# Softmax sums and running maxima on VectorE, taken over two columns of one operand in place of two operands

## The chip, the cores and the metric

The kernel runs on one core of a Trainium2 chip. A core has a matrix engine (TensorE, PE in the profile, with its weight loads as PEld), VectorE (DVE), ScalarE (ACT), GpSimd (POOL) and a queue that issues DMAs (SP). All work on SBUF, the core's memory of 128 partitions; TensorE writes to PSUM, which VectorE and ScalarE read. The metric is the device time of one execution in microseconds (us).

## The reference

Sliding-window attention with four sink tokens, over 4 batches, 8 heads, 768 positions and head size 64, followed by a soft mixture of experts over the 3072 tokens: 8 experts with 4 slots each.

```
scores = scale * q @ k^T
keep   = (key is one of the first 4) or (0 <= query - key < 128)
scores = where(keep, scores, -1e9)
a = exp(scores - max(scores))
a = a / (sum(a) + 1e-9)
x = a @ v                                   # 3072 tokens of 512

logits = x @ phi                            # 3072 x 32
d = exp(logits - logits.max(0));  d /= d.sum(0) + 1e-9
slot_out = relu(d^T @ x, per expert, @ w1) @ w2
c = exp(logits - logits.max(1));  c /= c.sum(1) + 1e-9
out = c @ slot_out
```

Two softmaxes matter here: that of the attention, one sum per query and head, and that over the tokens (`d`), whose maximum and sum run along as the tokens are made.

## The kernel before

The attention is cut into 12 jobs of 256 queries (4 batches times 3). Each job loads its keys, queries and values, transposes keys and queries on TensorE, and then works on four tiles; a tile covers 128 rows of queries (half of each 128) and four heads. For each tile, in `softmax`: TensorE makes the scores `s` in PSUM, VectorE masks them and takes the negated maxima `nm`, ScalarE takes the exponentials of the four heads in four instructions, each of which also reads out its sum, and VectorE makes the reciprocals: it adds the constant 1e-9 to the four sums (`inverse`, a `tensor_tensor` with the four-column tile `eps`) and inverts. GpSimd then multiplies the weights `pt` by them. TensorE transposes `pt`, ScalarE or VectorE copies the result out (`xw`), GpSimd's `affine_select` cuts it to the window, and TensorE multiplies by the values.

Each job then passes its 256 tokens on to `Moe.tokens`, the softmax over tokens with a running maximum: `logits` on TensorE, their maximum on VectorE (`new`, one column of the pair `m`, which alternates between jobs), the smaller of the new and the old negated maximum, exponentials on ScalarE, and then the running sum `z`, which VectorE multiplies by the factor `al` and to which it adds the job's own sum `zb` (`totals`). `slot_softmax` runs once a batch over `call`, the logits of that batch's tokens; its maxima are `rm` and its sums `rs`. After the last job come the two expert layers, whose weights are loaded from early on, and the output.

The order on each engine is fixed when the program is built. Each step is given to a list scheduler (`Plan.add`) with a key, an engine and an estimated time; the scheduler's order is the order in which each engine runs its instructions, and an engine waits at each instruction for what that instruction needs. Nearly every recorded instruction has line 127, the helper that records it, so the names of its tiles tell instructions apart: `wt<-wt 128x4` on VectorE are the attention's sums and reciprocals, since `wt` is the name of the shared slots in which `pt`, `small` and `eps` lie; `sums` is the tile that holds `m`, `z`, `zb` and `al`; `first` holds keys and queries, and the tokens `x` with their transposes.

Of the kernel before, what the change touches and what calls it, by code (L numbers as in the profile page):

```python
# [14 lines left out]
ALU = mybir.AluOpType  # L15
AX = mybir.AxisListType
# [6 lines left out]
EPS = 1e-9  # L23
# [254 lines left out]
class Moe:  # L278
# [27 lines left out]
    def tokens(self, plan, keys, b, j, x, xn, blocks):  # L306

        nc, c = self.nc, self.c
        n, self.n = self.n, self.n + 1
        old, new = self.m[:, (n + 1) % 2:(n + 1) % 2 + 1], self.m[:, n % 2:n % 2 + 1]
        lt, z, acc, xt = self.lt, self.z, self.acc, self.xt
        al, zb = (x[:, n % 2:n % 2 + 1] for x in (self.al, self.zb))
        aln, zbn = ("al", n % 2), ("zb", n % 2)
        lb, lg = self.lb[:, n % 2], self.call[:, b, 2 * j:2 * j + 2]
        both = len(blocks) == 2
        k = iter(keys)  # L320
        L, T, S = plan.psum(), plan.psum(), plan.psum()

        xs = [("xt", b, u) for b in blocks for u in range(2)]

        def logits(e):
            for a in range(4):
                for g in range(4):
                    nc.tensor.matmul(L["tile"][32 * g:32 * g + 32, 0:P], lhsT=c.phi[:, a, :],
                                     rhs=xt[:, a, x[g % 2 if both else blocks[0]]], start=(a == 0), stop=(a == 3),
                                     skip_group_check=True)  # L330

        plan.add(next(k), "P", 0.87, logits, r=xs + ["phi"], w=[L["name"]], new=L, mode=(128, 32))

        key = next(k)
        plan.add(key, "V", 0.2, lambda e: nc.vector.tensor_reduce(
            new, L["tile"][:, 0:P], op=ALU.max, axis=AX.X, negate=True), r=[L["name"]], w=[("m", n % 2)])
        if n:
            plan.add(key, "V", 0.07, lambda e: nc.vector.tensor_tensor(new, new, old, op=ALU.min),
                     r=[("m", (n + 1) % 2)], w=[("m", n % 2)])
        plan.add(next(k), "A", 0.16, lambda e: nc.scalar.copy(lt[0:64], L["tile"][0:64, 0:P]), r=[L["name"]], w=["lt0"])  # L340
        plan.add(next(k), "A", 0.34,
                 lambda e: nc.scalar.activation(lt[64:128], L["tile"][64:128, 0:P], AF.Exp, bias=new[64:128],
                                                accum_out=zb[64:128]),
                 r=[L["name"], ("m", n % 2)], w=["lt1", zbn], last=L)
        if n:

            plan.add(next(k), "A", 0.19,
                     lambda e: nc.scalar.activation(al, old, AF.Exp, bias=new, scale=-1.0),
                     r=[("m", 0), ("m", 1)], w=[aln])
        else:  # L350
            next(k)
        plan.add(next(k), "P", 0.11, lambda e: nc.tensor.transpose(T["tile"][:, 0:P], lt, c.ident),
                 r=["lt0", "lt1"], w=[T["name"]], new=T)
        i = slice(0, 2) if both else slice(blocks[0], blocks[0] + 1)

        def natural(e, w):
            t = T["tile"][:, 0:P].rearrange("p (w i s) -> p w i s", w=2, i=2)
            o, t = (lb, t[:, 1]) if w else (lg[:, i], t[:, 0, i])
            (nc.scalar.copy if e == "A" else nc.vector.tensor_copy)(o, t)

        plan.add(next(k), "AV", (0.1, 0.13), lambda e: natural(e, 1), r=[T["name"]], w=[("lb", n % 2)])
        logit = lambda e: natural(e, 0)

        def products(e):
            for g in range(4):
                i, o = g % 2, slice(256 * (g // 2), 256 * (g // 2) + 256)
                if both:
                    lhs, rhs = lb[:, i, :], xn[i][:, o]
                else:
                    rows = slice(64 * i, 64 * i + 64)  # L370
                    lhs, rhs = lb[rows, i, :], xn[blocks[0]][rows, o]
                nc.tensor.matmul(S["tile"][32 * g:32 * g + 32, 0:256], lhsT=lhs, rhs=rhs, start=True, stop=True)

        plan.add(next(k), "P", 0.45, products, r=[("lb", n % 2)] + [("xn", b) for b in blocks], w=[S["name"]], new=S,
                 mode=(128, 32))

        def sums(e):
            if n:
                nc.vector.scalar_tensor_tensor(acc, acc, al, S["tile"][:, 0:256], op0=ALU.mult, op1=ALU.add)
            else:  # L380
                nc.vector.tensor_copy(acc, S["tile"][:, 0:256])

        def totals(e):
            if not n:
                nc.vector.tensor_copy(z[64:128], zb[64:128])
            elif both:
                nc.vector.scalar_tensor_tensor(z[64:128], z[64:128], al[64:128], zb[64:128],
                                               op0=ALU.mult, op1=ALU.add)
            else:
                nc.vector.tensor_tensor(z[64:128], z[64:128], al[64:128], op=ALU.mult)  # L390
                nc.vector.tensor_tensor(z[64:96], z[64:96], zb[64:96], op=ALU.add)

        plan.add(next(k), "V", 0.14, totals, r=[zbn, aln], w=["z"])
        key = next(k)
        plan.add(next(k), "AV", (0.1, 0.13), logit, r=[T["name"]], w=[("lg", b, j, x) for x in blocks], last=T)
        plan.add(key, "V", 0.4, sums, r=[S["name"], aln], w=["acc"], last=S)
# [259 lines left out]
def window_path(ctx, tc, c, moe, q, k, v, phi, w1, w2, out):  # L656
# [6 lines left out]
    nc = moe.nc = Core(tc)  # L663
    B, H, S, D = q.shape
    NJ = S // 256
    plan = Plan(moe.pools)
# [5 lines left out]
    def slot():  # L672
        return slots.tile([P, 2048], F32, name="wt")

    t, u = moe.first
# [7 lines left out]
    t = slot()  # L683
# [3 lines left out]
    t = slot()  # L687
    pts = [t[:, 528 * i:528 * i + 528].rearrange("p (a y) -> p a y", a=4) for i in range(PT)]
    skb = t[:, 1584:1840].rearrange("p (i r h s) -> p i r h s", i=2, r=4, h=H)
    small = t[:, 1840:1864].rearrange("p (g x y) -> p g x y", g=3, x=2)  # L690
    eps = t[:, 1864:1868]
    v4s.append(t[:, 1868:1932])
    qt = fr.tile([P, 4, 256], F32, name="qt")
    vsink = fr.tile([P, 4, P], F32R, name="vsink")
    pst = fr.tile([P, 256], F32R, name="pst")
    nc.vector.memset(eps, EPS)

    jobs = [(b, j) for b in range(B) for j in range(NJ)]
    N = len(jobs)
# [75 lines left out]
    def softmax(keys, n, tl):  # L775

        b, j = jobs[n]
        g = 4 * n + tl
# [3 lines left out]
        nm, z = small[:, g % 3, 0], small[:, g % 3, 1]  # L782
# [43 lines left out]
        def exps(e):  # L826
            for a in range(4):
                nc.scalar.activation(pt[:, a, :], used[0][:, a % 2, a // 2, :], AF.Exp, bias=nm[:, a:a + 1],
                                     accum_out=z[:, a:a + 1])

        add(keys["E"], "A", 1.42, exps, r=[sn, nn], w=[pn, zn], last=s)

        def inverse(e):
            nc.vector.tensor_tensor(z, z, eps, op=ALU.add)
            nc.vector.reciprocal(z, z)

        add(keys["N"], "V", 0.33, inverse, r=[zn], w=[zn])
        add(keys["N"], "G", 1.08, lambda e: nc.gpsimd.tensor_tensor(
            pt, pt, z.unsqueeze(2).to_broadcast([P, 4, 132]), op=ALU.mult), r=[zn, pn], w=[pn])
# [297 lines left out]
def fused(ctx, tc, q, k, v, n_sink, window, phi, w1, w2, out):  # L1137
# [42 lines left out]
    with tc.If(flag == 1) as cmp:  # L1180
        with ExitStack() as c2:
            window_rest(tc, moe, *window_path(c2, tc, c, moe, q, k, v, phi, w1, w2, out), out)
# [33 lines left out]
```

## Time and profile before

| | |
|---|---|
| time, median of 3 runs | 254.32 us (253.89 to 254.34) |
| profiled execution, span | 252.0 us |
| mean granted clock of TensorE in it | 0.966 |
| instructions on VectorE, busy | 445, 171.3 us |
| instructions on GpSimd, busy | 281, 143.2 us |
| loaded and stored | 59.38 MB |

The page gives the profiled execution by its span, from the first to the last instruction; the runs' times are taken of the whole execution, and are 2.3 us above it in the median. The twelve jobs run from about 9 us to 196 us; every third job begins a batch, and one batch takes about 44 us. The expert layers and the output take the rest.

The costliest groups of GpSimd, and the two groups of VectorE that are largest (columns: line, engine, operation, written and read tiles, shapes, count; busy us and mean ns of one; idle time of the engine before them and what ended it):

```profile
L127 POOL TENSOR_TENSOR wt<-wt 128x528 f32<-128x528 f32 (+1 forms) x96 | 64.4, 677 | 14.4 <-DVE wt L127 8.4
L127 POOL TENSOR_SCALAR_AFFINE_SELECT wt<-wt 128x512 f32<-128x512 f32 x88 | 53.6, 638 | 20.8 <-DVE wt L127 12.0
L127 DVE TENSOR_REDUCE wt<-s 128x4 f32<-128x528 f32 x48 | 34.0, 707 | 1.7
L127 DVE COPY_PREDICATED s<-later,s 128x256 f32<-128x256 uint8 x48 | 20.3, 423 | 2.7 <-PE s L127 2.0
```

Busy time of an engine counts from an instruction's start to its end, and so also what it stands still in between; idle time is what lies between instructions.

### The profile page before, as it was taken

To read this page: it belongs to the slowest core of one execution; us is meant where nothing else is said; L and a number is where in the kernel's file an instruction comes from. 1 tells how busy PE (TensorE), PEld (TensorE's weight loads), DVE (VectorE), ACT (ScalarE), POOL (GpSimd) and SP (SyncE) were. 2 spreads that over 40 slices of the span, in tenths; PEclk is the share of its full clock that TensorE was granted. 3 is DMA by queue.
4 is the path that set the end of the run, shared out by engine and by line. 5 is a ranking of instruction groups with operands and counts; after the bars stand their busy time and mean duration, and the time that the engine had idled before them with its cause. 6 is when DMAs were issued, how large, how long until landed. Compare 5 with 4: busy or idle time off the path is not lost.

```text
span 252.0 us, 7482 instructions
## 1 busy us (share of the span) xinstructions
PE 225.1 (89%) x2754; PEld 162.0 (64%) x2754; DVE 171.3 (68%) x445; ACT 143.7 (57%) x568; POOL 143.2 (57%) x281
## 2 busy tenths in 40 slices
PE   7969899989998999999899899998999999997900
PEld 7746677857786786778678677876677434335800
DVE  3297879788889978888997888898554413104810
ACT  2368887558786665879666587975545112103700
POOL 2038897955958596595859659596884060000000
PEclk9979999999999999999999999999999999998865
DMA  5597899799799799969988982640159999950995
GB/s 117 111 205 171 172 290 275 239 275 283 232 217 257 229 300 272 279 218 208 271 314 217 279 252 50 137 151 5 37 193 347 349 414 423 410 213 23 388 395 207
DMA packets 84495, 59.38 MB, mean 236 GB/s; under 512 B 76260, under 2 KB 76260, under 8 KB 82916
## 3 DMA queue, kind: packets, MB, share of 16 engines
q1 hardware_dynamic: 84452, 58.83, 78.1%
q8 instruction: 24, 0.39, 0.6%
q14 instruction: 19, 0.16, 0.2%
HBM read 52.53 MB, written 6.29 MB: 233 GB/s over the span
## 4 chain that ended last, share of the span: by engine, by line
PE 56%; DVE 22%; ACT 9%; issue 5%; POOL 2%; DVEq 0%; ACTq 0%; POOLq 0%
PE w L127 42%; PE s L127 13%; DVE wt L127 10%; ACT wt L127 7%; DVE s L127 7%; POOL wt L127 2%; PE w L1168 2%; DVE sums L127 1%; DVE rs L127 1%; DVE call L127 1%; ACT lt L127 1%; DVE acc L127 1%; DVE wt L579 0%; ACT qt L127 0%; ACT wt L578 0%
## 5 line engine op out<-in xcount | busy, mean ns | idle before, releaser
L127 POOL TENSOR_TENSOR wt<-wt 128x528 f32<-128x528 f32 (+1 forms) x96 | 64.4, 677 | 14.4 <-DVE wt L127 8.4
L127 ACT ACTIVATE wt<-s,wt 128x132 f32<-128x132 f32 x192 | 68.4, 386 | 6.9 <-DVE wt L127 6.1
L127 POOL TENSOR_SCALAR_AFFINE_SELECT wt<-wt 128x512 f32<-128x512 f32 x88 | 53.6, 638 | 20.8 <-DVE wt L127 12.0
L127 PE MATMUL w<-wt 128*64 128x128 f32 (+3 forms) x550 | 51.9, 320 | 1.6 <-DVE wt L579 1.5
L127 PEld LDWEIGHTS w<-wt 128*64 128x64 f32 (+2 forms) x550 | 37.3, 144 | 13.5 <-DVE wt L579 2.2
L127 PE MATMUL s<-wt,qt 64*64 64x196 f32 (+2 forms) x768 | 41.4, 327 | 4.2 <-ACT wt L127 3.2
L127 PE MATMUL w<-ident,first 128*128 128x128 f32 x288 | 41.6, 281 | 2.4 <-DVE acc L127 1.3
L127 ACT ACTIVATION_READ_ACCUMULATOR wt<-s,wt 128x1 f32 x192 | 42.6, 222 | 0.0
L127 ACT COPY wt<-w 128x512 f32<-128x512 f32 x45 | 26.6, 595 | 25.5 <-PE w L127 22.1
L127 PE MATMUL w<-ident,wt 128*128 128x128 f32 x250 | 39.0, 283 | 1.6 <-ACT lt L127 0.8
L127 PEld LDWEIGHTS w<-ident,first 128*128 128x128 f32 x288 | 31.8, 142 | 9.7 <-issue 3.9
L127 PEld LDWEIGHTS s<-wt,qt 64*64 64x64 f32 x768 | 26.6, 134 | 14.7 <-issue 7.4
L127 DVE TENSOR_REDUCE wt<-s 128x4 f32<-128x528 f32 x48 | 34.0, 707 | 1.7
L127 PEld LDWEIGHTS w<-ident,wt 128*128 128x128 f32 x250 | 27.9, 146 | 9.9 <-POOL wt L127 2.9
L127 DVE TENSOR_TENSOR wt<-wt 128x4 f32<-128x4 f32 x48 | 16.4, 342 | 12.0 <-ACT wt L127 11.1
L127 ACT COPY first<-w 128x512 f32<-128x512 f32 x31 | 17.9, 596 | 8.4 <-PE w L127 8.2
L127 DVE COPY_PREDICATED s<-later,s 128x256 f32<-128x256 uint8 x48 | 20.3, 423 | 2.7 <-PE s L127 2.0
L127 DVE COPY wt<-w 128x512 f32<-128x512 f32 x27 | 18.3, 679 | 2.1 <-PE w L127 1.7
L127 PE MATMUL w<-first,phi 128*32 128x128 f32 x384 | 13.1, 276 | 2.0 <-DVE first L127 1.9
L127 POOL COPY wt<-wt 128x512 f32<-128x512 f32 (+2 forms) x13 | 5.8, 455 | 15.0 <-ACT wt L127 14.9
L127 PE MATMUL w<-wt,si 128*32 128x512 f32 x128 | 13.9, 593 | 0.2 <-DVE si L127 0.2
L127 PE MATMUL s<-wt 128*32 128x512 f32 (+1 forms) x144 | 14.0, 498 | 0.0
(116 smaller groups left out, 240.8 us busy)
## 6 DMA issues: line engine op xcount, KB each, us to landing
wt<-in_moe_w_dram SPq DMA_DIRECT2D x30, 1024.0 KB, 7.4
wt<-in_v_dram SPq DMA_DIRECT2D x24, 256.0 KB, 4.9
first<-in_k_dram SPq DMA_DIRECT2D x22, 256.0 KB, 3.7
first<-in_q_dram SPq DMA_DIRECT2D x22, 256.0 KB, 4.4
out_dram<-wt SPq DMA_DIRECT2D x5, 1024.0 KB, 8.3
first<-in_moe_w_dram SPq DMA_DIRECT2D x2, 1024.0 KB, 5.0
out_dram<-wt SPq DMA_DIRECT2D x2, 512.0 KB
first<-in_k_dram SPq DMA_DIRECT2D x4, 128.0 KB, 2.3
```

The lines of the kernel that those rows point to most:

```text
L127: return self.tc.keep_in_program_order(f(*args, **kw))
L1168: nc.tensor.matmul(t[:, 0:P], lhsT=c.ident, rhs=c.ident, start=True, stop=True)
```

## The change

Three operations of VectorE are written in another form; what is computed stays the same.

1. The attention's sums. ScalarE writes its sums into a new tile `ze`, which has two columns for each sum: the sum itself and, set once, the constant 1e-9. VectorE sums both columns of each pair with one `reduce_sum` (8 values in, 4 out), in place of adding the tile `eps` to the tile of sums. This occurs 48 times, once a tile.
2. The running maximum. The smaller of the two negated maxima is taken by one `tensor_reduce` over both columns of `m`, in place of a `tensor_tensor` of the two columns. This occurs 11 times.
3. The running sum. `z * al + zb` is one `tensor_scalar` with two scalars per partition, in place of a `scalar_tensor_tensor` whose addend is a tensor. This occurs 11 times.

```diff
-            plan.add(key, "V", 0.07, lambda e: nc.vector.tensor_tensor(new, new, old, op=ALU.min),
+            plan.add(key, "V", 0.07, lambda e: nc.vector.tensor_reduce(new, self.m, op=ALU.min, axis=AX.X),
                      r=[("m", (n + 1) % 2)], w=[("m", n % 2)])
...
-                nc.vector.scalar_tensor_tensor(z[64:128], z[64:128], al[64:128], zb[64:128],
-                                               op0=ALU.mult, op1=ALU.add)
+                nc.vector.tensor_scalar(z[64:128], z[64:128], al[64:128], zb[64:128], op0=ALU.mult, op1=ALU.add)
...
     small = t[:, 1840:1864].rearrange("p (g x y) -> p g x y", g=3, x=2)
-    eps = t[:, 1864:1868]
+    ze = t[:, 1932:1956].rearrange("p (g y e) -> p g y e", g=3, e=2)
...
-    nc.vector.memset(eps, EPS)
+    nc.vector.memset(ze[:, :, :, 1], EPS)
...
                 nc.scalar.activation(pt[:, a, :], used[0][:, a % 2, a // 2, :], AF.Exp, bias=nm[:, a:a + 1],
-                                     accum_out=z[:, a:a + 1])
+                                     accum_out=ze[:, g % 3, a, 0:1])
...
         def inverse(e):
-            nc.vector.tensor_tensor(z, z, eps, op=ALU.add)
+            nc.vector.reduce_sum(z, ze[:, g % 3], axis=AX.X)
             nc.vector.reciprocal(z, z)
```

The keys and the estimated times of the steps are as before, and with them the order on all engines. As an example, VectorE's instructions around a slot softmax, first before the change (`rm`, `call` and `rs` are of the slot softmax, the rows `wt<-wt 128x4` of the attention's sums):

```order
L127 TENSOR_REDUCE rm<-call 128x6
L127 TENSOR_TENSOR call<-call,rm 128x192
L127 TENSOR_TENSOR wt<-wt 128x4
L127 RECIPROCAL wt<-wt 128x4
L127 COPY first_77<-w 128x512
L127 COPY wt<-w 128x2x4x64
```

At the same place with the change, on VectorE too:

```order
L127 TENSOR_REDUCE rm<-call 128x6
L127 TENSOR_TENSOR call<-call,rm 128x192
L127 TENSOR_REDUCE wt<-wt 128x4
L127 RECIPROCAL wt<-wt 128x4
L127 COPY first_77<-w 128x512
L127 COPY wt<-w 128x2x4x64
```

Nothing has moved; one row has another operation.

## Prediction

> **What bounds the kernel now.** I read the page first, then the windows, then the instructions in order of time.
>
> ```profile
> span 252.0 us, 7482 instructions
> PE 225.1 (89%) x2754; PEld 162.0 (64%) x2754; DVE 171.3 (68%) x445; ACT 143.7 (57%) x568; POOL 143.2 (57%) x281
> PE 56%; DVE 22%; ACT 9%; issue 5%; POOL 2%; DVEq 0%; ACTq 0%; POOLq 0%
> ```
>
> TensorE holds 56% of the chain that ended last, VectorE 22%. Where VectorE's part lies is told by the windows (busy us of each engine in a stretch).
>
> ```profile
> core 0: us, PE busy (x) PEld busy (x) DVE busy (x) ACT busy (x) POOL busy (x), PEclk, DMA share, GB/s
> 58.50:73.90 15.40, 15.40 (x211) 12.51 (x213) 13.39 (x32) 11.97 (x52) 11.64 (x21) 1.00 0.95 244
> 73.90:85.00 11.10, 10.31 (x158) 7.38 (x157) 9.97 (x28) 6.90 (x34) 9.79 (x19) 1.00 0.91 253
> 91.40:102.60 11.20, 10.63 (x143) 8.01 (x139) 9.94 (x27) 6.89 (x28) 7.26 (x16) 1.00 0.99 313
> 118.00:129.00 11.00, 10.22 (x158) 7.30 (x156) 9.87 (x28) 6.81 (x34) 9.75 (x19) 1.00 0.90 254
> ```
>
> From 58.5 to 73.9 TensorE has no idle time at all: nothing saved on VectorE can shorten that stretch. From 73.9 to 85.0 and, one batch later, from 118.0 to 129.0, TensorE idles 0.79 and 0.78 us (length minus busy), and VectorE is busy for nine tenths. So the change can win at most what TensorE idles, stretch by stretch, and only where VectorE makes it idle.
>
> **The change, part by part.** The three edited operations of before, and their nearest relatives among the reductions (columns: xcount | busy us, mean ns | idle before):
>
> ```profile
> L127 DVE TENSOR_TENSOR wt<-wt 128x4 f32<-128x4 f32 x48 | 16.4, 342 | 12.0 <-ACT wt L127 11.1 <-POOL wt L127 0.4
> L127 DVE TENSOR_TENSOR sums<-sums 128x1 f32<-128x1 f32 x11 | 2.3, 207 | 0.2
> L127 DVE SCALAR_TENSOR_TENSOR sums<-sums 64x1 f32<-64x1 f32 x11 | 2.4, 220 | 0.8 <-ACT lt L127 0.5
> L127 DVE TENSOR_SCALAR rz<-sums,f,eps 128x1 f32<-128x1 f32 x1 | 0.3, 270 | 0.0
> L127 DVE TENSOR_REDUCE low<-ident 128x1 f32<-128x64 f32 x1 | 0.2, 196 | 0.0
> L1178 DVE TENSOR_REDUCE same<-same 1x1 int32<-1x4 int32 x1 | 0.1, 145 | 0.0
> L51 DVE TENSOR_REDUCE slot<-ident 128x32 f32<-128x128 f32 x1 | 0.3, 350 | 0.0
> ```
>
> An addition over four columns should not take 342 ns. The instructions in order of time show why it does: three on VectorE, then three on GpSimd.
>
> ```profile
> 75.58 0.76 DVE L127 TENSOR_TENSOR wt<-wt 128x4 f32<-128x4 f32 x1 [0.76 <-ACT wt L127]
> 80.45 0.59 DVE L127 TENSOR_TENSOR wt<-wt 128x4 f32<-128x4 f32 x1
> 82.34 0.15 DVE L127 TENSOR_TENSOR wt<-wt 128x4 f32<-128x4 f32 x1
> 75.25 1.07 POOL L127 TENSOR_TENSOR wt<-wt 128x528 f32<-128x528 f32 x1
> 78.51 2.51 POOL L127 TENSOR_SCALAR_AFFINE_SELECT wt<-wt 128x512 f32<-128x512 f32 x4
> 81.40 1.07 POOL L127 TENSOR_TENSOR wt<-wt 128x528 f32<-128x528 f32 x1 [0.38 <-DVE wt L127]
> ```
>
> The first starts inside a GpSimd multiplication that ends at 76.32 and itself ends at 76.34; the second starts inside a run of four GpSimd selects that ends at 81.02, and itself ends at 81.04; the third comes only 0.13 us before the multiplication from 81.40 ends at 82.47, and takes 0.15 us. So an addition with two operands in SBUF stands until GpSimd's current instruction ends, and 0.15 us is its own price. Of the 16.4 us, 48 x 0.15 = 7.2 are work and 9.2 are standing.
>
> Does a reduction stand too? Two instructions that follow each other in the slot softmax, four times each, answer (min/median/max ns):
>
> ```profile
> L127 DVE TENSOR_REDUCE rm<-call x4: 344/353/353, 79.6 to 197.2; 128x6 f32<-128x192 f32 x4
> L127 DVE TENSOR_TENSOR call<-call,rm x4: 359/554/557, 80.0 to 197.6; 128x192 f32<-128x192 f32 x4
> ```
>
> The one at 79.6 lies inside the selects from 78.51, as does its neighbour at 80.0; at 197 GpSimd is idle. The two-operand subtraction goes from 359 to about 555 ns, the reduction from 344 to 353. A reduction of one operand does not wait. The Trainium skill says the same (page "SBUF — State Buffer", section "Who interferes with whom"): a VectorE instruction with two SBUF inputs contends with a GpSimd instruction that reads SBUF, and tensor_reduce on trn2 never does; the trace agrees, 555 against 353 ns.
>
> What will the new reduction of 8 into 4 values take? From below 145 ns (the four-element row), from above 350 (the 128-element row with strided reading); 64 elements take 196, so 8 lie near the lower end. I take 150, no different from the addition's 0.15. The minimum of two columns likewise: 207 becomes about 150, 0.6 us over 11. The sum z*al+zb in its new form is nearest to the rz row, 270 against 220: 11 x 0.05 = 0.55 us more, behind the exponentials where VectorE then copies for TensorE's next transposes; should that cover go, it costs those 0.55 us. ScalarE's sums now go to every second column, still one column per write, so I take no difference there (nothing in the trace writes both ways; a few ns on 192 reads would show on ScalarE, which is busy 57%). The memset grows from 4 to 12 columns, once. No instruction changes its place and no wait is added: each sum still waits for ScalarE's four accumulators, and GpSimd's multiplication for the reciprocal behind it. VectorE thus loses some 9 us of standing, spread over twelve jobs; now which of it sits on the path.
>
> **Place A**, the stretches from 73.9 and from 118.0, each with one slot softmax. Standing goes at 75.58 (0.76 to 0.15, 0.61) and 80.45 (0.59 to 0.15, 0.44). What waits for it:
>
> ```profile
> 76.46 0.66 DVE L127 COPY wt<-w 128x512 f32<-128x512 f32 x1
> 81.16 0.66 DVE L127 COPY first<-w 128x512 f32<-128x512 f32 x1
> 81.88 1.08 PE L127 MATMUL w<-first,phi 128*32 128x128 f32 x32 [0.66 <-DVE first L127]
> ```
>
> VectorE runs from 75.58 to 81.82 with few gaps, then TensorE starts. VectorE would arrive up to 1.05 us earlier; TensorE idles only 0.79 in the window. From below, if the work behind the copy at 76.46 comes to wait for TensorE's scores instead, only the second counts, 0.4. I take 0.75, twice: **1.5 us** (0.8 to 1.6). Late next is TensorE itself.
>
> **Place B**, from 38 to 53:
>
> ```profile
> 38.07 1.02 DVE L127 TENSOR_TENSOR wt<-wt 128x4 f32<-128x4 f32 x1
> 45.45 0.91 DVE L127 TENSOR_TENSOR wt<-wt 128x4 f32<-128x4 f32 x1 [0.85 <-ACT wt L127]
> 42.45 0.66 PE L127 MATMUL w<-ident,first 128*128 128x128 f32 x4 [0.40 <-ACT lt L127]
> 51.27 0.44 PE L127 MATMUL w<-ident,wt 128*128 128x128 f32 x2 [0.42 <-ACT call L127]
> 52.86 0.41 PE L127 MATMUL w<-first,phi 128*32 128x128 f32 x6 [0.32 <-DVE first L127]
> ```
>
> 0.87 and 0.76 us of standing, with 0.40 + 0.42 + 0.32 = 1.14 us of TensorE idle behind them. The exponentials on ScalarE lie between, and the scores from TensorE; at least the first gap should go. I take **0.9** (0.4 to 1.14).
>
> **Place C**, the third slot softmax:
>
> ```profile
> 164.20 0.45 DVE L127 TENSOR_TENSOR wt<-wt 128x4 f32<-128x4 f32 x1
> 168.17 0.59 DVE L127 TENSOR_TENSOR wt<-wt 128x4 f32<-128x4 f32 x1
> 171.03 0.99 DVE L127 TENSOR_SCALAR rs<-rs 128x6 f32<-128x6 f32 x1
> L127 DVE TENSOR_SCALAR rs<-rs x4: 172/172/987, 83.0 to 198.9; 128x6 f32<-128x6 f32 x4
> 173.34 1.09 PE L127 MATMUL w<-ident,wt 128*128 128x128 f32 x8 [0.81 <-ACT lt L127]
> ```
>
> 0.30 + 0.44 go, and TensorE idles 0.81. But the 0.99 us belong to an unchanged instruction that takes 172 ns in the median of its four: how long it stands depends on what GpSimd does just then, and a shift may shorten or lengthen that. I take **0.6** (0.2 to 0.81).
>
> **Place D**, the running minimum of the last but one job:
>
> ```profile
> 183.18 0.65 DVE L127 TENSOR_TENSOR sums<-sums 128x1 f32<-128x1 f32 x1
> 184.69 0.33 PE L127 MATMUL w<-ident,lt 128*128 128x128 f32 x1 [0.25 <-ACT lt L127]
> ```
>
> 0.50 go, 0.25 is idle: **0.2** (0 to 0.25). In 91.4 to 102.6 the idle 0.57 us stays, for the sums just ahead and there have nothing to lose:
>
> ```profile
> 90.20 0.20 DVE L127 TENSOR_TENSOR wt<-wt 128x4 f32<-128x4 f32 x1 [0.76 <-ACT wt L127]
> ```
>
> After 197 no edited instruction is left.
>
> Sum: 1.5 + 0.9 + 0.6 + 0.2 = **3.2 us**, from 1.4 to 3.8 with the ends. The page gives the profiled execution as its span, 252.0; the runs' median is 254.32, and I let the 2.3 us between them stand. Forecast: span 248.8, time 254.3 - 3.2 = **251.1 us**.
>
> **Rivals.** *The standing moves.* The two-operand instructions that stay keep meeting GpSimd, and VectorE arriving earlier may stand there instead.
>
> ```profile
> L127 DVE TENSOR_TENSOR call<-call,rs x4: 349/602/850, 83.5 to 199.3; 128x192 f32<-128x192 f32 x4
> ```
>
> For it: this product of the slot softmax, 349 to 850 ns, lies in places A and C, as does the 0.99 us row. Against: GpSimd waits for the same reciprocals and shifts along. If each of the three loses 0.5 us (850 less 349), the sum falls from 3.2 to 1.7; if B also gives only its 0.4, to 1.2: between 252.6 and 253.1, say 252.9.
>
> *More comes back.* If all idle time of TensorE outside 58.5 to 73.9 and its like shrank, also the 0.57 us of the windows from 91.4 once in each of three batches (1.7 us), and the ends above were met (3.8), 5.5 us would go; 5 leaves about 249.3. Against it: those gaps follow memsets and maxima that the change does not touch.
>
> *It is hidden.* TensorE is busy 89% of the span; if another wait, on ScalarE's exponentials above all (the row at 42.45 names ScalarE), fills each gap, the time stays within 0.2% (0.5 us, about what a measurement of this kernel can tell from no change): 254.1.
>
> *The reduction itself is slow.* One mechanism: two values per output, read in groups, at the strided row's 350 ns or more. Between 75.58 and 85 three sums lie in VectorE's run, so with d ns over 150 place A loses 3d. It decides at about d = 350 (3 x 0.35 = the 1.05 us won there), a reduction of 500 ns; at 600 ns A loses 0.3 twice, the sums around 91.4 to 102.6 with nothing to win lose 2 x 0.45 in each of three batches, and B still wins 0.87 + 0.76 - 2 x 0.45 = 0.7: 254.3 + 0.6 + 2.7 - 0.7 = 256.9. The Trainium skill warns in this direction (page "VectorE: DVE Perf Modes", section "Rules for kernel authors"): it calls tensor_reduce the slowest operation and advises restructuring it away. The rows of 145 and 196 ns speak against that at 8 elements.
>
> **How the numbers follow.** Forecast (249.9 to 252.2) 0.55; standing moves 0.19; more comes back 0.13; hidden 0.08; slow reduction 0.05. Faster by over 0.2%: 0.55 + 0.19 + 0.13 = 0.87; within 0.08; slower 0.05. The range takes the forecast, the standing rival and half of the generous one, 249.0 to 253.5; what is left out holds 0.2.
>
> **What would show it.** Right: the 48 sums as reductions at about 150 ns each with no tail, VectorE's busy time some 9 us lower, TensorE's wait at the place of 81.88 and its like one batch later gone, the window from 58.5 as long as before. Wrong: reductions of 300 ns and more; or waits of the same length on the slot softmax's rows; or TensorE idling as long, now released by ScalarE. The forecast also fails if the last weights land no earlier than before while TensorE comes to them sooner.

## The result and the profile after

| | before | after |
|---|---|---|
| time, median | 254.11 us (253.89 to 254.34, 4 runs) | 249.59 us (248.95 to 249.93, 4 runs) |
| ratio, 95% interval | | 0.983 (0.980 to 0.986) |
| span of the profiled execution | 252.0 us | 247.8 us |

The changed kernel is 4.5 us faster by the medians, 3.6 to 5.1 by the interval; the two profiled executions lie 4.2 apart. Four of all the executions on record, three of the kernel before and one of an experiment, were slow ones of 266 us or more, which every ratio here leaves out. From the page after, the span, the engines and the chain's shares by engine:

```profile
span 247.8 us, 7482 instructions
PE 223.9 (90%) x2754; PEld 163.1 (66%) x2754; DVE 161.9 (65%) x445; ACT 142.9 (58%) x568; POOL 143.0 (58%) x281
PE 66%; DVE 17%; ACT 7%; issue 3%; DMA 1%; POOL 0%; ACTq 0%; DVEq 0%; POOLq 0%
```

VectorE is busy 9.4 us less with as many instructions, and of the chain that ended last it holds 17% in place of 22%, TensorE 66% in place of 56%. TensorE is busy 1.2 us less, with the same instructions (225.1 before), so of the 4.2 us between the two spans 3.0 were idle time of TensorE and 1.2 were counted as busy. The edited operations, from the groups of VectorE by form (xcount | busy us, mean ns | idle before):

```profile
L127 DVE TENSOR_REDUCE wt<-wt 128x4 f32<-128x8 f32 x48 | 7.5, 156 | 12.1 <-ACT wt L127 9.9 <-POOL wt L127 1.7
L127 DVE TENSOR_REDUCE sums<-sums 128x1 f32<-128x2 f32 x11 | 1.6, 148 | 0.2
L127 DVE TENSOR_SCALAR sums<-sums 64x1 f32<-64x1 f32 x11 | 3.0, 276 | 0.6 <-ACT lt L127 0.2
```

In the mean a sum takes 156 ns where it took 342, a minimum 148 where it took 207, and `z*al+zb` 276 where it took 220. The windows of the two places A, about the same work as in the prediction's windows and with the same columns:

```profile
72.40:82.70 10.30, 10.30 (x160) 7.55 (x158) 9.22 (x30) 7.41 (x37) 9.54 (x17) 1.00 0.96 256
115.50:126.00 10.50, 10.50 (x161) 7.75 (x161) 9.39 (x30) 7.57 (x37) 9.93 (x18) 1.00 1.00 272
```

TensorE has no idle time left there, where it had 0.79 and 0.78 us.

**Where the time went.** TensorE runs the same 2754 instructions in both kernels, so one can be followed through both profiles: its start before, less its start after, is TensorE's lead. For example, the first matmul of the row that started at 81.88 in the kernel before (TensorE in order of time, after):

```profile
80.39 1.08 PE L127 MATMUL w<-first,phi 128*32 128x128 f32 x32
```

The lead is 81.88 - 80.39 = 1.49 us there. The same difference for this kernel and for those of the experiments below, taken from their profiles at the first TensorE instruction that started at or behind the time at the column's head in the kernel before:

```
lead of TensorE, us       38     55     73     82   84.9     90    117    134    160    176    186    229
whole change           -0.18   0.82   0.76   1.49   1.78   2.10   2.05   3.39   3.33   4.13   4.42   4.09
changed kernel again   -0.59   0.41   0.35   1.08   1.37   1.68   1.62   2.94   2.87   3.64   3.92   3.88
sums alone              0.27   1.27   1.25   1.99   1.84   1.83   1.84   2.40   2.40   3.18   3.19   3.18
minima and z alone     -0.18  -0.21  -0.27  -0.35  -0.33  -0.39  -0.45  -0.57  -0.63  -0.60  -0.33  -0.36
eight sums              0.25   1.23   1.24   1.97   1.66   1.65   1.66   2.05   2.06   2.49   2.50   2.50
the other forty         0.46   0.44   0.42   0.40   0.40   0.40   0.39   0.36   0.36   0.59   0.86   0.83
sums and minima        -0.42   0.58   0.58   1.31   1.60   2.00   2.01   3.43   3.44   4.21   4.48   4.11
no additions            0.24   1.43   1.37   2.10   2.39   2.71   2.87   4.21   4.35   5.63   6.29   5.50
each sum twice         -0.16   0.64   0.58   1.30   0.94   0.89   0.64   0.94   0.68   0.79   1.05   1.02
four sums, minima       0.21   0.23   0.23   0.96   0.66   0.66   0.68   1.10   1.10   1.16   1.44   1.41
eight sums, minima     -0.33   0.66   0.67   1.40   1.10   1.10   1.10   1.53   1.54   1.97   2.25   2.09
six sums, minima       -0.30  -0.32  -0.32   0.41   0.71   1.12   1.14   2.57   2.57   2.60   2.87   2.83
```

The first column is scatter of the start-up, which one profile alone cannot tell from an effect; the steps along a row are what counts. For the whole change: 1.00 at place B (38 to 55), 1.34 at each place A (73 to 90 and 117 to 134), 0.80 at C (160 to 176), 0.29 at D (176 to 186), and -0.33 at the last weights (186 to 229). The sum is 4.44; small losses in between take 0.17 of it, so that the lead rises by 4.27 in all. A second profile of the changed kernel repeats the first five steps to 0.03 us (1.00, 1.33, 1.32, 0.77, 0.28), but loses only 0.04 at the last weights.

In place A, VectorE's rows after, in order of time, and then two of GpSimd's:

```profile
74.82 0.16 DVE L127 TENSOR_REDUCE wt<-wt 128x4 f32<-128x8 f32 x1 [0.70 <-ACT wt L127]
79.16 0.15 DVE L127 TENSOR_REDUCE wt<-wt 128x4 f32<-128x8 f32 x1
80.61 0.15 DVE L127 TENSOR_REDUCE wt<-wt 128x4 f32<-128x8 f32 x1
81.75 0.42 DVE L127 TENSOR_TENSOR call<-call,rs 128x192 f32<-128x192 f32 x1
82.09 0.14 DVE L127 TENSOR_REDUCE sums<-sums 128x1 f32<-128x2 f32 x1
```

```profile
81.70 0.25 POOL L127 TENSOR_TENSOR wt<-wt 128x32 f32<-128x32 f32 x1
81.91 1.18 POOL L127 TENSOR_TENSOR wt<-wt 128x528 f32<-128x528 f32 x1
```

And the last two of VectorE's and the last of GpSimd's in the kernel before:

```profile
83.46 0.85 DVE L127 TENSOR_TENSOR call<-call,rs 128x192 f32<-128x192 f32 x1
84.23 0.16 DVE L127 TENSOR_TENSOR sums<-sums 128x1 f32<-128x1 f32 x1
```

```profile
83.03 1.07 POOL L127 TENSOR_TENSOR wt<-wt 128x528 f32<-128x528 f32 x1
```

The first two sums lose 0.60 and 0.44 us, as worked out (0.61 and 0.44). The third was not standing before (0.15) and does not now. But the product of the slot softmax, which the change does not touch, went from 0.85 to 0.42: 0.43 us that the forecast's sum has not. Before, it started 0.43 us behind the start of GpSimd's multiplication of 528 columns and stood while that ran; now it starts 0.16 us ahead of it. TensorE's transposes behind it, before and after:

```profile
84.15 1.88 PE L127 MATMUL w<-ident,first 128*128 128x128 f32 x12
85.86 0.66 PE L127 MATMUL w<-ident,wt 128*128 128x128 f32 x4
86.36 1.14 PE L127 MATMUL w<-ident,first 128*128 128x128 f32 x8
```

```profile
82.66 1.53 PE L127 MATMUL w<-ident,first 128*128 128x128 f32 x12
84.03 0.60 PE L127 MATMUL w<-ident,wt 128*128 128x128 f32 x4
84.46 1.04 PE L127 MATMUL w<-ident,first 128*128 128x128 f32 x8
```

The same instructions, at a granted clock of 1.00 both times, take 0.35, 0.06 and 0.10 us less. The first row before joins matmuls over a gap of 0.13 us in front of 84.93, which is the rest of the window's 0.79 us of idle time (0.66 stands at 81.88). The other 0.38 us lay inside what is counted as TensorE's busy time, where the idle columns do not show them.

### The profile page after: what moved, and what is told of

Same layout as the page of the kernel before. It is cut to its first block, busy times and chain, and to the rows that moved or that the text cites. A ratio compares the mean times of both kernels' runs of the same rounds, so it can differ in the third digit from the quotient of the medians.

```text
span 247.8 us, 7482 instructions
## 1 busy us (share of the span) xinstructions
PE 223.9 (90%) x2754; PEld 163.1 (66%) x2754; DVE 161.9 (65%) x445; ACT 142.9 (58%) x568; POOL 143.0 (58%) x281
## 4 chain that ended last, share of the span: by engine, by line
PE 66%; DVE 17%; ACT 7%; issue 3%; DMA 1%; POOL 0%; ACTq 0%; DVEq 0%; POOLq 0%
PE w L127 48%; PE s L127 17%; DVE s L127 6%; DVE wt L127 6%; ACT wt L127 5%; PE w L1167 2%; DMA out_dram<-wt 1%; ACT wt L592 1%; DVE sums L127 1%; DVE call L127 1%; DVE acc L127 1%; DVE first L127 1%; DVE wt L578 0%; ACT qt L127 0%; ACT wt L577 0%
## 5 line engine op out<-in xcount | busy, mean ns | idle before, releaser
L127 PE MATMUL w<-ident,first 128*128 128x128 f32 x288 | 41.0, 280 | 1.7 <-DVE sums L127 0.9
L127 DVE TENSOR_REDUCE wt<-wt 128x4 f32<-128x8 f32 x48 | 7.5, 156 | 12.1 <-ACT wt L127 9.9
L127 DVE TENSOR_SCALAR qt<-w 128x512 f32<-128x512 f32 x20 | 12.9, 681 | 0.6 <-PE s L127 0.5
```

The costliest lines, as they stand in the source:

```text
L127: return self.tc.keep_in_program_order(f(*args, **kw))
```

## Experiments

**The sums alone.** The minima and `z` stay as before.

```diff
+    ze = t[:, 1932:1956].rearrange("p (g y e) -> p g y e", g=3, e=2)
+    nc.vector.memset(ze[:, :, :, 1], EPS)
...
-                                     accum_out=z[:, a:a + 1])
+                                     accum_out=ze[:, g % 3, a, 0:1] if one else z[:, a:a + 1])
...
-            nc.vector.tensor_tensor(z, z, eps, op=ALU.add)
+            if one:
+                nc.vector.reduce_sum(z, ze[:, g % 3], axis=AX.X)
+            else:
+                nc.vector.tensor_tensor(z, z, eps, op=ALU.add)
```

with `one = True`.

> Only the 48 attention sums as reductions; the running minimum and z*al+zb as before. Theory (a two-operand instruction stands until GpSimd's current one ends, a reduction does not; the 48 sums carry nearly all of it): 249.8 us, 0.2 to 0.4 above the whole change, because the minimum at 183 keeps its 0.65 us. Rival (the change of the accumulator column or the other two edits carry a share): over 251.

Measured: 251.21 us (250.55 to 251.55), ratio 0.990 (0.988 to 0.992). A miss: it lies 1.6 us above the whole change, where the rival put it. Place A, VectorE and then GpSimd in order of time:

```profile
81.25 0.37 DVE L127 TENSOR_TENSOR call<-call,rs 128x192 f32<-128x192 f32 x1
81.54 1.02 DVE L127 TENSOR_TENSOR sums<-sums 128x1 f32<-128x1 f32 x1
```

```profile
81.36 1.18 POOL L127 TENSOR_TENSOR wt<-wt 128x528 f32<-128x528 f32 x1
```

The minimum took 0.16 us at this place in the kernel before. Here it stands 1.02 us, until GpSimd's multiplication ends at 82.54. The product just ahead of it, which has two operands too, starts 0.11 us before that multiplication and does not stand; the minimum starts 0.18 us behind its start, and has inherited the standing of the sums that were freed. TensorE's transposes come to wait behind it (0.28 us at 83.10 for ScalarE's `lt`, which itself waits for the minimum): the lead falls by 0.15 between 82 and 85, and a place A ends at 0.58 or 0.56 in place of 1.34.

**The minima and `z` alone.** Parts 2 and 3 of the change, without the sums; the lines are those of the change's diff.

> Only the minimum and z*al+zb in the new form; the 48 sums as before. Theory: the minimum at 183 falls from 0.65 to 0.15 us, TensorE's wait of 0.25 behind it goes, and the 11 sums z*al+zb cost 0.06 us each with no effect: 253.9 us, 0.2 below before and at most 0.4. Rival (the other two edits carry a share of the 4.5 us): below 253.

Measured: 254.22 us (253.11 to 254.75), ratio 1.001 (0.999 to 1.003). By itself this half is worth nothing that can be measured (the theory had 0.2 us), though D shows its 0.27 in the table. What it is worth beside the sums, the run with sums and minima below tells.

**Eight sums, and the other forty.** The sums' edit with `one = g in (9, 11, 19, 20, 31, 32, 43, 44)`, the tiles that the prediction's places A, B and C name, and with `one = g not in` that list.

> Reductions for 8 of the 48 sums only: those that stood in the places A, B and C of the prediction (tiles 9, 11, 19, 20, 31, 32, 43, 44 in the order of the run; 4.4 of the 9.2 us of standing). Theory (only what stands in VectorE's run ahead of a TensorE wait counts): nearly the whole gain, TensorE 0.9 + 1.3 + 1.3 + 0.8 us earlier, 250.0 to 250.6 us. Rival (the gain follows VectorE's total of standing): about half, 252.0 us.

> Reductions for the other 40 sums (4.8 of the 9.2 us of standing); those 8 as before. Theory: TensorE has no idle time behind these, so 253.8 to 254.1 us. Rival (the gain follows VectorE's total): about 251.9 us.

Measured: the eight 251.46 us (251.06 to 251.97), ratio 0.991 (0.989 to 0.994); the forty 253.36 us (252.79 to 253.76), ratio 0.998 (0.996 to 0.999). Both miss the theory's figures: the eight lie between the two accounts, 0.9 us above 250.6 and 0.5 below 252.0, and the forty 0.4 below 253.8. But halves of the standing are far from worth the same, 2.4 us and 0.5, so nearly all that the sums give without the minima (2.7) comes from eight of them. The forty give 0.23 at C and 0.27 at D and nothing in A, where the first two sums still stand.

**The changed kernel again**, for the scatter between chips, no edit.

> The changed kernel once more, beside the kernels of this group on one chip. Both theories: 4.3 us below before (the first measurement's ratio, 0.980 to 0.986).

Measured: 249.63 us (248.60 to 250.13), ratio 0.982 (0.978 to 0.987).

**Sums and minima, `z` as before**: the first two parts of the change.

> The 48 sums and the 11 minima as reductions, z*al+zb as before. Theory (with the sums alone, the standing moves on to the minimum behind the slot softmax: 0.16 us before, 1.02 in that trace; the minimum as a reduction frees 0.6 to 0.7 us at each of two places and 0.25 at 183): within 0.3 us of the whole change, about 249.6. Rival (z*al+zb is the other partner, or the shortfall of the sums alone was the measurement): 251 or more, as with the sums alone.

Measured: 249.40 us (248.62 to 249.81), ratio 0.982 (0.978 to 0.986). This is the whole change's time, as the theory had it. The sums alone give 2.7 us, the minima (with `z`) alone nothing, both together 4.7: the minima are worth what the sums would otherwise lose at them, 2.0 us by the medians and 1.6 by the leads. The new form of `z`, 56 ns longer each time, neither helps nor costs anything that can be measured; in the kernel before, none of the eleven stood (219 to 221 ns each).

**One operand and a number.** The kernel before, with the sum as `tensor_scalar`, which has one operand in SBUF. It asks whether one operand is enough.

```diff
-            nc.vector.tensor_tensor(z, z, eps, op=ALU.add)
+            nc.vector.tensor_scalar(z, z, EPS, None, op0=ALU.add)
```

> The kernel before, with the 48 sums taken as one operand plus an immediate constant (tensor_scalar 128x4, the form of the row rs, 172 to 987 ns), no second operand. Theory (what counts is whether the form stands when GpSimd runs, and this form does): mean near 340 ns, 253.5 to 254.3 us, no gain. Rival (one operand in place of two is what counts): mean near 170 ns and 251.2 us, as with the sums alone.

Measured: 254.15 us (253.19 to 255.00), ratio 1.000 (0.998 to 1.002). The group by form:

```profile
L127 DVE TENSOR_SCALAR wt<-wt 128x4 f32<-128x4 f32 x48 | 17.0, 353 | 12.0 <-ACT wt L127 11.1 <-POOL wt L127 0.4
```

353 ns in the mean, as much as with two operands (342), and no gain: this form stands too, as the theory had it. The Trainium skill (page "SBUF — State Buffer", section "Who interferes with whom") names `tensor_scalar` among the operations that can take the port pair shared with GpSimd, and `tensor_reduce` as the one that on trn2 never does. The two rows, 353 and 156 ns, agree with it. What sets them apart here is the operation, not the number of operands that the prediction spoke of.

**No additions at all.** The changed kernel, with the reciprocals taken straight of ScalarE's sums and of the slot softmax's.

```diff
-            nc.vector.tensor_scalar(rs, rs, EPS, None, op0=ALU.add)
...
-            nc.vector.reduce_sum(z, ze[:, g % 3], axis=AX.X)
-            nc.vector.reciprocal(z, z)
+            nc.vector.reciprocal(z, ze[:, g % 3, :, 0])
```

> The changed kernel without its 1e-9: VectorE inverts the attention's sums directly (the 48 reductions of 0.156 us are left out), and the same constant is left out of the slot softmax's sums (4 times 0.17 us). The sums are at least 1, where 1e-9 is below the last digit of f32. Theory (VectorE is the wait of TensorE in few places by now: 2.2 us of its waits before 197 are still released by VectorE): 0.4 to 1.0 us below the changed kernel, about 248.9. Rival (VectorE no longer sets the end anywhere): 249.6, as the changed kernel.

Measured: 248.03 us (247.16 to 248.87), ratio 0.976 (0.972 to 0.981), the fastest of all, 1.6 us below the changed kernel by the medians (1.0 by the rise of the leads), where 0.4 to 1.0 was expected: VectorE still holds TensorE up in places. In the table its lead over the kernel before falls by 0.79 us between 186 and 229, where the changed kernel's falls by 0.33. TensorE's row there names a load of the last weights, with 0.15 us as idle time:

```profile
220.30 2.78 PE L127 MATMUL s<-wt 128*32 128x256 f32 x44 [0.15 <-DMA wt<-in_moe_w_dram]
```

**Each sum twice.** The changed kernel with the reduction done two times, to price a slow one.

```diff
             nc.vector.reduce_sum(z, ze[:, g % 3], axis=AX.X)
+            nc.vector.reduce_sum(z, ze[:, g % 3], axis=AX.X)
```

> The changed kernel with each of the 48 reductions done twice: 48 x 0.19 us (0.156 and the step to the next instruction) = 9.1 us more on VectorE, as if the reduction took 0.35 us. Theory (the prediction's rival of the slow reduction, worked with d = 0.19: three sums in each of two places A, two around each of three places with nothing to win, two in B, two in C): 0.19 x (6 + 6 + 2 + 2) = 3.0 us, 252.6 us. Rival (VectorE has so much idle time by now that this is hidden): 249.6 to 250.2 us.

Measured: 253.72 us (252.50 to 254.75), ratio 0.999 (0.997 to 1.002). That is 4.1 us for 48 more reductions, above the 3.0 expected. The profiled execution is one of the faster ones (252.72): by its lead, which rises by 1.18 and not by 4.27, it loses 3.1. Place A, VectorE and then GpSimd (x2 is the doubled sum, 0.35 us where one takes 0.15):

```profile
80.99 0.35 DVE L127 TENSOR_REDUCE wt<-wt 128x4 f32<-128x8 f32 x2
...
82.30 1.08 DVE L127 TENSOR_TENSOR call<-call,rs 128x192 f32<-128x192 f32 x1
```

```profile
82.10 1.07 POOL L127 TENSOR_TENSOR wt<-wt 128x528 f32<-128x528 f32 x1
```

Each reduction more costs about 0.2 us, but VectorE now reaches the product 0.20 us behind the start of GpSimd's multiplication, and the product takes 1.08 us in place of 0.42. The places A shrink from 1.34 to 0.31 and 0.30, C from 0.80 to 0.11 and B from 1.00 to 0.80; another 0.25 goes between the two places A and between the second and C. The theory's total fits the profile's, but its parts do not: it had 0.57 for each place A, where 1.03 went.

**Four sums and the minima; eight sums and the minima.** These ask whose the surplus of place A is. With the minima as reductions, the sums' edit has `one = g in (19, 20, 31, 32)`, the first two sums of each place A, or the eight tiles from above.

> The kernel before with the running minima as reductions, and of the 48 sums only four as reductions: tiles 19 and 20 (the two of the first place A) and 31 and 32 (the two of the second). It asks whose the surplus of place A is (1.33 and 1.29 us in the whole change, where 0.75 each was forecast). Theory, A is local: its two sums and the minimum behind them give it all, about 2.6 us together, and the waits of TensorE on the copies from 84.9 to 87.6 shorten too: 254.1 - 2.6 = 251.5 us (251.2 to 251.9), TensorE's lead over the kernel before rises by about 1.3 us between 80 and 88 and again between 122 and 132, and stays as it is elsewhere. Rival, A draws on the sums ahead of it, which let VectorE come to 73.9 earlier: A gives 0.75 to 0.8 each, 252.5 to 252.6 us.

> The kernel before with the running minima as reductions, and of the 48 sums the eight of places A, B and C (tiles 9, 11, 19, 20, 31, 32, 43, 44). Theory, what counts is local to places A to D: A 2.6, B 0.9, C 0.3 (the forty others gave 0.37 there by themselves), D 0.25, less 0.2 to 0.3 at the last weights: 254.1 - 3.8 = 250.3 us (249.9 to 250.7). Rival, the forty other sums matter once the minimum no longer stands: 251.2 us or more, near the 251.5 us of the eight alone.

Measured: four 252.57 us (nine runs, 251.70 to 253.09), ratio 0.995 (0.993 to 0.997); eight 251.55 us (250.17 to 252.74), ratio 0.991 (0.988 to 0.994). Both times lie where the rivals put them, but with four the agreement is luck: a place A gives 0.43 us, where the theory had 1.3 and the rival 0.75 to 0.8. The rows with four, VectorE and then GpSimd, show why, and it is neither theory:

```profile
79.64 0.15 DVE L127 TENSOR_REDUCE wt<-wt 128x4 f32<-128x8 f32 x1
...
81.09 0.76 DVE L127 TENSOR_TENSOR wt<-wt 128x4 f32<-128x4 f32 x1
...
82.81 0.86 DVE L127 TENSOR_TENSOR call<-call,rs 128x192 f32<-128x192 f32 x1
```

```profile
80.76 1.06 POOL L127 TENSOR_TENSOR wt<-wt 128x528 f32<-128x528 f32 x1
```

The third sum of the place, which took 0.15 us in the kernel before, now comes early enough to meet GpSimd's multiplication, and stands until it ends. Behind it the product stands as before. With eight, the third sums are also among those that keep two operands, and a place A gives 0.43 as well. With four, the 0.73 us won at 82 fall back to 0.43.

**Six sums and the minima.** The third sum of each place A as well: `one = g in (19, 20, 21, 31, 32, 33)`.

> The run with four sums (tiles 19, 20, 31, 32) and the minima as reductions, and the third sum of each place A as well (tiles 21 and 33). With four, the third sum took over the standing: 0.76 us, ending with GpSimd's multiplication, where it took 0.15 before, and the product of the slot softmax behind it stood 0.86 us as before; in the whole change these two take 0.15 and 0.42. Theory, the standing is handed from one two-operand instruction to the next, and A's surplus comes when the last of the chain is free of it: with the third sum as a reduction VectorE reaches the product earlier, the product takes about 0.42 us, and TensorE's lead rises by 1.3 us at each place A: 254.0 - 2.6 = 251.4 us (251.0 to 251.8). Rival, A's surplus needs the sums of the stretches ahead (58 to 74), which this kernel leaves as they were: as with four, 252.4 to 252.7 us.

Measured: 250.61 us (250.36 to 251.69), ratio 0.988 (0.985 to 0.990), 0.4 us below the theory's range and far from the rival. VectorE in place A:

```profile
81.64 0.15 DVE L127 TENSOR_REDUCE wt<-wt 128x4 f32<-128x8 f32 x1
...
82.82 0.38 DVE L127 TENSOR_TENSOR call<-call,rs 128x192 f32<-128x192 f32 x1
83.13 0.14 DVE L127 TENSOR_REDUCE sums<-sums 128x1 f32<-128x2 f32 x1
```

Each place A gives 1.44 and 1.43 us, with the sums of the stretches ahead as they were. Six sums of 48 and the minima carry 3.4 of the 4.5 us, more than the 2.6 expected, which left out D; by the leads they are 1.44 + 1.43 + 0.27 = 3.1. Two sums that did not stand in the kernel before are worth 1.0 us each (1.44 against 0.43).

## Why the prediction was right, and where it was not

The mechanism held. The sums stood behind GpSimd, as reductions they do not (147 to 165 ns, all 48), and TensorE's idle time ended by VectorE fell from 3.7 to 2.4 us between 9 and 197, that ended by ScalarE from 6.5 to 5.1; the window from 58.5 to 73.9 gave nothing (0.82 at 55, 0.76 at 73).

The size did not hold as well. The time, 249.6, lies in the range, but 1.5 us below the forecast of 251.1 (0.2 of it because the kernel before came out at 254.11 and not at 254.32), and below the 249.9 at which the prediction's own band begins; the upper end of its sum was 3.8 us, and 4.5 was measured. The range holds the time because it took in half of "More comes back", which had 249.3. That rival's extra mechanism did not happen: the gaps of the window from 91.4 stay (0.57 us idle before, 0.58 in the same work after), and the lead falls by 0.05 between 90 and 117. That the range held is in part luck.

By the terms of the sum:

- **The price of a reduction**, taken as 150 ns: 156 and 148. **`z*al+zb`**, taken as 270: 276, and hidden. **ScalarE's sums** into every second column, taken as no difference: its reads of the sums take 223 ns in the mean of 192, where they took 222.
- **Place B**, taken as 0.9 (0.4 to 1.14): 1.00. **D**, taken as 0.2: 0.29, a little over its bound of 0.25.
- **Place C**, taken as 0.6: 0.80. The standing of the unchanged row at 171.03 (0.99) did shift, as was feared. Now that group and the product's read, by tile (min/median/max ns):

```profile
L127 DVE TENSOR_SCALAR rs<-rs x4: 171/171/172, 81.2 to 194.4; 128x6 f32<-128x6 f32 x4
L127 DVE TENSOR_TENSOR call<-call,rs x4: 359/418/1134, 81.8 to 194.9; 128x192 f32<-128x192 f32 x4
```

  The 0.99 us have gone. In their place the product stands, until GpSimd's multiplication ends, which started 0.14 us ahead of it. The product's row before and after, and GpSimd's after:

```profile
172.32 0.35 DVE L127 TENSOR_TENSOR call<-call,rs 128x192 f32<-128x192 f32 x1
```

```profile
167.46 1.13 DVE L127 TENSOR_TENSOR call<-call,rs 128x192 f32<-128x192 f32 x1
```

```profile
167.32 1.07 POOL L127 TENSOR_TENSOR wt<-wt 128x528 f32<-128x528 f32 x1
```

  The 0.82 us that left the one row and the 0.78 that came to the other cancel, and C gives about what its own two sums stood, 0.30 + 0.44.
- **Place A is the term that was mis-sized**: 0.75 each with a bound of 0.8, measured 1.34 each, 1.2 us too little in all. Two steps of its working failed. The first is the cap, "TensorE idles only 0.79 in the window" with "Late next is TensorE itself". At the instruction of 81.88 the lead did rise by 0.73, just what was forecast. Then 0.29 came at 84.9 and 0.32 up to 90. Of the 1.34 us of the first place A only the 0.79 were idle time; the other 0.55 were short waits inside what is counted as TensorE's busy time, in the window and behind its end. The second is that only the standing of the edited sums was counted. The product behind them lost 0.43, and the third sum, entered at nothing because it took 0.15 us, is worth 1.0 us: had it kept its two operands, it would have taken over the standing of the two ahead, as the run with four sums shows.
- **"The standing moves"** was the rival that described this. In C it named the right instruction, the product, but there the unchanged row lost as much. In A it had the wrong instructions and one sign only: it looked at those that stay unedited, and the product came free there. Its counter-argument, that GpSimd shifts along, held in part only: in the first place A GpSimd's multiplication came 1.12 us earlier and the product 1.71. In the whole change the minimum and the third sum are edited too, so in A the chain ends free of standing. In the sums alone, the eight and the four it did happen: at the minimum (1.02 us) and at the third sum (0.76 us).
- **"The reduction itself is slow"** was given a break-even of 500 ns. Doing it twice costs 4.1 of the 4.5 us by the medians, at 0.19 us a sum; so by an estimate from that run a reduction of about 0.35 us would have been the point. The price of 3d per place A (0.57 us for d = 0.19) left out the product, which stands again; 1.03 was measured.
- **The last weights**: the lead falls from 4.42 to 4.09 behind 186. The prediction said that the forecast fails if they land no earlier. They came earlier, but not by as much as TensorE did: in the traces the last part of the load lands at 225.60 before and at 221.66 after, and the first matmul that waits for it starts at 225.79 and 221.71, 0.3 us later than the lead of 4.42 would have it. The second profile of the changed kernel loses 0.04 there, so the loss differs from one execution to the next; without the additions it is 0.79. No run moved those loads.

## What to carry to other kernels

Where one engine stands behind another, price the chain and not the instruction: list every instruction behind the first one that can stand, edited or not, and ask what each will meet when it comes earlier. A duration without standing is no proof that an edit there is worth nothing, and half of such a change can be worth far less than its share. The idle time of the engine that waits is no upper bound on the gain, since it also waits for short spells inside what the profile counts as busy, and behind the window's end.

## What the runs showed of the hardware that was not expected

- An addition of a number to four columns (`tensor_scalar`, one operand in SBUF) stands behind GpSimd as an addition of two tiles does: 353 against 342 ns in the mean of 48, while a reduction of eight columns into four takes 156.
- The product of 192 columns and GpSimd's multiplication of 528 columns hold each other up, and which of them stands goes by which starts first. In the changed kernel the product starts at 81.75, 0.16 us ahead: it takes 0.42 us, and the multiplication 1.18 where it takes 1.07 in the kernel before. With each sum twice the product starts 0.20 us behind: it takes 1.08, and the multiplication 1.07. In the traces of all fourteen runs the products that start ahead of such a multiplication take 0.36 to 0.44 us, and those that start while one runs 0.84 to 1.14. The Trainium skill says so (page "SBUF — State Buffer", section "Who interferes with whom": the order of issue decides who blocks), and the rows agree.
- A minimum of two single columns, which takes 0.15 us undisturbed, stood for 1.02 us in the run with the sums alone.
